# Weight conversion in the head: six one-input steps on GpSimd instead of VectorE, loads and head steps in another order

## The chip, the cores and the metric

The kernel runs on one core of a Trainium2 chip. The metric is the device time in microseconds (us) of one execution; smaller is better. TensorE (PE), VectorE (DVE), ScalarE (ACT), GpSimd (POOL) and SyncE (SP) each work through their own list of instructions in order; SP issues the transfers. A wait at the front of a list holds everything behind it.

## What is computed

An induced attention block over `x` (4 batches of 12544 tokens, 128 channels, float32), followed by a maxout layer with weights of 128 x 768. Cut to what matters:

```
def mab(q, kv):                      # softmax attention
    s = scale * (q @ kv.T); s -= s.max(-1)
    a = exp(s); a /= a.sum(-1) + 1e-9
    return a @ kv
h = mab(inducing, x)                 # 32 induced points per batch, over all 12544 tokens
y = mab(x, h)                        # every token against the 32 points
hid = maximum(maximum(y @ w1, y @ w2), y @ w3)
out = hid @ w_out
```

The four weights are float64. Each is brought to the chip as pairs of 32-bit words and converted there.

## The kernel before

**Two stages.** The *head* treats batch 0 up to the first products of the maxout layer; a main loop of slots follows, in which the maxout layer of one 512-token chunk after another is worked off while later batches' attention runs beside it. The order of every engine's instructions is that in which the code emits them; no scheduler changes it. In the head that order is the string `HEAD`: each word is a step, and a step appends its instructions to the lists of its engines.

**Loads.** The tokens of batch 0 come in seven groups: group 0 is short (2 tiles of 128 tokens), groups 1 to 6 have 16 tiles (1 MB) each. `LOADS` is the order in which SP issues them with the four weights (0.75 MB each; w_out is `wo`). Group 1 and group 6 are loaded in four pieces of 4 tiles.

**Head steps of batch 0.** For group g and piece k, `T:g.k` transposes four tiles on PE into a PSUM bank, `c:g.k` (ACT) or `C:g.k` (DVE) copies it to SBUF. `S:g` is the score product on PE, `M:g` its maximum (DVE), `D:g` spreads it (ACT), `G:g` sums it over partitions (PE), `L:g` takes the least (DVE), `E:g` the exponential (ACT), `R:g` a 32x32 transpose (DVE), `U:g` the product with the tokens (PE), `H:g` / `HV:g` its copy out of PSUM (ACT / DVE), `K:g` a copy of one column (POOL). Groups 0 and 1, 2 and 3, 5 and 6 share one maximum, so `G:5` waits for `M:6`. After the last group: `least`, `wts`, `lw` (the groups' weights), `maskp`, `y`, `tot`, `rec` and `hT`, the 32 induced points; from `hT` come the scores of the first chunks (`parts`, then the softmax steps `p:w.n`) and the first combined weights (`up`, `hi`, `lov`, `lop`).

**Weight conversion.** Weight k (0 is w2, 1 is w_out, 2 is w1, 3 is w3) passes through
`n:k` (ACT, absolute value of the high words), `r:k` (scale the low words), `m:k` (a lower bound), `i:k` (a shift by 3), `v:k` (POOL, integer sum of the two), `d:k` (DVE, put the sign back; two inputs from SBUF). `r`, `m` and `i` have one input and stand on DVE before. `e:k.part.parts` subtracts w2 from w1 or w3 on DVE, `ep` does it on POOL. The tiles of `n` (`size`) and of `r` (`rest`) have two buffers each, so the third weight's `r` waits for the first weight's `d`. `N` and `F` are products that nobody reads.

Of the kernel before, what the change touches and what calls it, by code (L numbers as in the profile page):

```python
# [26 lines left out]
def kernel(ctx, tc, x, xt, ind_t, w1, w2, w3, w_out, out):  # L27
    nc = tc.nc
    B, N, C = x.shape
    M = ind_t.shape[1]  # L30
# [15 lines left out]
    HEAD = """
        n:0 r:0 F:17 T:1.1 T:1.0 m:0 i:0 C:1.0 c:1.1 T:1.2 c:1.2 T:1.3 C:1.3 T:0.0 S:1 c:0.0 S:0 M:1 M:0 D:1 D:0 v:0
        d:0 T:2.2 C:2.2 T:2.3 c:2.3 T:2.0 c:2.0 G:1 L:1 K:0 T:2.1 C:2.1 E:1 T:3.3 E:0 c:3.3 T:3.2 T:3.0 c:3.0 T:3.1
        n:2 C:3.2 R:1 r:2 m:2 R:0 i:2 c:3.1 S:2 M:2 U:1 S:3 M:3 U:0 HV:1 T:4.1 C:4.1 v:2 D:2 D:3 T:4.2 c:4.2 G:2 L:2
        E:2 d:2 R:2 e:2.0.1 T:4.3 T:4.0 c:4.0 c:4.3 E:3 R:3 T:5.2 c:5.2 n:3 S:4 M:4 D:4 r:3 m:3 i:3 K:3 v:3 U:2  # L50
        T:5.0 c:5.0 T:5.1 c:5.1 G:4 L:4 E:4 T:5.3 C:5.3 T:6.0 C:6.0 T:6.2 c:6.2 T:6.1 c:6.1 R:4 T:6.3 c:6.3 S:5 d:3
        M:5 S:6 M:6 U:3 n:1 m:1 r:1 D:5 D:6 G:5 L:5 K:6 i:1 v:1 H:2 U:4 E:5 e:3.0.2 R:5 E:6 least R:6 H:4 w2T U:5
        U:6 wts lw maskp tot H:5 y:1 y:2 w2h d:1 woh wol y:4 y:5 rec hT parts:0 parts:2 e:3.1.2 p:0.0 p:0.1 p:0.2
        p:0.3 p:2.0 up:0 up:1 hi:0 hi:1 lop:1 p:0.4 p:0.5 p:2.1 p:0.6 p:0.7 up:2 hi:2 mw p:2.2 p:2.3 cw p:0.8 turn:0
        pca:0 turn:1 pca:1 lov:0 lov:2 p:2.4 s:0 up:3 hi:3 N:1 s:1 s:2 p:2.5 N:1 s:3 s:4 p:2.6 N:1 s:5 next p:2.7
        x:0 lov:3 s:6 p:2.8 q:0 q:1 x:1 q:2 q:3 q:4 q:5 q:6 q:7
    """
# [43 lines left out]
    def load_group(b, gi, pieces=1):
        g = groups[gi]
        if g["nt"] == GT:
            xg = xgs_free.pop(0) if xgs_free else xts_free.pop().rearrange("p (t c) -> p t c", c=C)
        else:
            xg = short_x
        n = g["nt"] // pieces
        for k in range(0, g["nt"], n):
            nc.sync.dma_start(out=xg[:, k : k + n, :], in_=xv[b, :, g["t0"] + k : g["t0"] + k + n, :])
# [73 lines left out]
    def weight_size(k):  # L183
# [5 lines left out]
    def weight_rest(k):
# [1 line left out]
        low = raws[k].rearrange("p (k two) -> p two k", two=2)[:, 0, :]
        nc.vector.tensor_scalar(out=rests[k], in0=low, scalar1=2.0**-51, scalar2=2.0, op0=ALU.mult, op1=ALU.add)

    def weight_least(k):
        nc.vector.tensor_scalar(out=sized[k], in0=sized[k], scalar1=LEAST, scalar2=None, op0=ALU.max)
# [973 lines left out]
```

## Time and profile before

| | |
|---|---|
| median of 3 runs | 809.62 us (809.48 to 809.74) |
| span of the profiled execution, first to last instruction | 807.8 us |
| what lies around the span | 1.85 us to the median; the profiled execution's own time is not listed apart |
| PE busy in the span | 799.0 us (99%) |
| DVE, ACT, POOL busy | 647.2, 714.4, 656.7 us (80%, 88%, 81%) |
| granted TensorE clock | 1.000 |
| head, to the first slots of the loop | about the first 48 us |

Idle time counts only on the engine that others wait for; of PE's idle time nearly all lies in the first 50 us. Times in the views are counted from the first instruction.

### The profile page before, as it was taken

To read this page: it belongs to the slowest core of one execution; us is meant where nothing else is said; L and a number is where in the kernel's file an instruction comes from. 1 tells how busy PE (TensorE), PEld (TensorE's weight loads), DVE (VectorE), ACT (ScalarE), POOL (GpSimd) and SP (SyncE) were. 2 spreads that over 40 slices of the span, in tenths; PEclk is the share of its full clock that TensorE was granted. 3 is DMA by queue.
4 is the path that set the end of the run, shared out by engine and by line. 5 is a ranking of instruction groups with operands and counts; after the bars stand their busy time and mean duration, and the time that the engine had idled before them with its cause. 6 is when DMAs were issued, how large, how long until landed. Compare 5 with 4: busy or idle time off the path is not lost.

```text
span 807.8 us, 15028 instructions
## 1 busy us (share of the span) xinstructions
PE 799.0 (99%) x4565; PEld 629.1 (78%) x4565; DVE 647.2 (80%) x1193; ACT 714.4 (88%) x1435; POOL 656.7 (81%) x637
## 2 busy tenths in 40 slices
PE   8999999999999999999999999999999999999998
PEld 6677778777787787787777877877778778777886
DVE  5988778779787797797976977978878878878874
...
GB/s 351 195 101 201 185 170 104 139 140 98 158 178 111 146 121 151 141 108 177 127 184 101 118 155 132 110 125 128 56 110 71 66 78 67 75 77 79 60 80 52
DMA packets 45408, 101.47 MB, mean 126 GB/s; under 512 B 9360, under 2 KB 15376, under 8 KB 40208
## 3 DMA queue, kind: packets, MB, share of 16 engines
...
q10 hardware_dynamic: 144, 0.13, 0.0%
...
## 4 chain that ended last, share of the span: by engine, by line
PE 95%; DMA 2%; ACT 1%; DVE 0%; issue 0%; SPq 0%; DVEq 0%
PE acc L942 50%; PE pu L848 16%; PE pv L854 16%; PE aux L730 3%; PE acc L936 3%; DMA xg<-in_x_dram 2%; PE acc L488 2%; PE aux L391 2%; PE aux L297 0%; PE acc L370 0%; PE aux L692 0%; ACT ru L863 0%; PE pv L281 0%; PE pu L281 0%; ACT a L336 0%
## 5 line engine op out<-in xcount | busy, mean ns | idle before, releaser
L878 POOL TENSOR_TENSOR lo<-h,hi 128x512 fp32r<-128x512 f32 (+1 forms) x498 | 621.2, 1277 | 111.3 <-ACT hi L870 54.7
L886 DVE TENSOR_TENSOR h<-pv,ru 128x512 f32<-128x512 f32 (+1 forms) x512 | 342.6, 672 | 129.3 <-PE pv L854 104.6
L863 ACT ACTIVATE ru<-pu 128x512 f32<-128x512 f32 (+1 forms) x600 | 368.2, 614 | 66.2 <-PE pu L848 61.9
L870 ACT CAST hi<-h 128x512 fp32r<-128x512 f32 (+1 forms) x512 | 320.1, 625 | 1.1 <-PE acc L942 0.7
L942 PE MATMUL acc<-hi,wo_hi 128*128 128x512 f32 (+1 forms) x601 | 234.8, 391 | 0.0
L848 PE MATMUL pu<-pT,us 128*128 128x512 f32 (+1 forms) x600 | 232.0, 387 | 0.3 <-ACT ru L863 0.2
L854 PE MATMUL pv<-pT,us 128*128 128x512 f32 (+1 forms) x600 | 231.6, 386 | 0.0
L942 PE MATMUL acc<-hi,wo_lo 128*128 128x512 f32 (+1 forms) x601 | 231.4, 385 | 0.0
L942 PE MATMUL acc<-lo,wo_hi 128*128 128x512 f32 (+1 forms) x601 | 231.3, 385 | 0.0
L942 PEld LDWEIGHTS acc<-hi,wo_hi 128*128 128x128 f32 x601 | 112.8, 188 | 41.3 <-issue 19.7
L848 PEld LDWEIGHTS pu<-pT,us 128*128 128x128 f32 x600 | 112.6, 188 | 24.3 <-issue 0.8
L854 PEld LDWEIGHTS pv<-pT,us 128*128 128x128 f32 x600 | 112.6, 188 | 23.5 <-DVE h L886 0.3
L942 PEld LDWEIGHTS acc<-lo,wo_hi 128*128 128x128 f32 x601 | 112.8, 188 | 22.9
L942 PEld LDWEIGHTS acc<-hi,wo_lo 128*128 128x128 f32 x601 | 112.9, 188 | 21.7
L886 DVE TENSOR_TENSOR aux<-pv,ru 128x512 f32<-128x512 f32 x66 | 45.7, 693 | 9.8 <-PE pv L854 3.5
L889 DVE TENSOR_TENSOR lo<-aux,hi 128x512 fp32r<-128x512 f32 x66 | 45.3, 686 | 1.4 <-PE acc L942 0.8
L870 ACT CAST hi<-aux 128x512 fp32r<-128x512 f32 x66 | 41.7, 632 | 0.1
L954 ACT COPY shelf<-acc 128x512 f32<-128x512 f32 (+1 forms) x65 | 39.1, 602 | 0.0
L936 PE MATMUL acc<-pT,us 128*128 128x512 f32 (+1 forms) x100 | 38.8, 388 | 0.0
L432 POOL COPY mq<-mq 32x1 f32<-32x1 f32 (+2 forms) x108 | 20.4, 189 | 5.2
L730 PE MATMUL aux<-xT,hT 128*32 128x512 f32 x184 | 24.5, 605 | 0.0
L488 PEld LDWEIGHTS acc<-xg,aT 128*32 128x32 f32 x576 | 16.8, 110 | 8.5 <-issue 7.8
...
## 6 DMA issues: line engine op xcount, KB each, us to landing
out_dram<-shelf SPq DMA_DIRECT2D x95, 256.0 KB, 2.0
...
```

What stands on the lines that cost most here:

```text
L488: nc.tensor.matmul(out=st["h"][q * M : (q + 1) * M, :], lhsT=aT[:, t * M : (t + 1) * M], rhs=row, start=(t < NQ), stop=(t + NQ >= len(rows)),)
L730: nc.tensor.matmul(out=sp[q * M : (q + 1) * M, :w], lhsT=st["hT"][:, :M], rhs=xT[:, q * w : (q + 1) * w], start=True, stop=True)
L848: nc.tensor.matmul(out=pu[:, :w], lhsT=state[c.b]["us"][:, 2 * j * P : (2 * j + 1) * P], rhs=c.pT[:, :w], start=True, stop=True)
L854: nc.tensor.matmul(out=pv[:, : d.w], lhsT=state[d.b]["us"][:, (2 * j + 1) * P : (2 * j + 2) * P], rhs=d.pT[:, : d.w], start=True, stop=True,)
L863: nc.scalar.activation(out=ru[:, :w], in_=pu[:, :w], func=AF.Relu)
L870: nc.scalar.copy(out=hi[:, : c.w], in_=h[:, : c.w])
L878: nc.gpsimd.tensor_sub(**args)
L886: nc.vector.tensor_max(out=h[:, : d.w], in0=pv[:, : d.w], in1=relus.pop(s)[:, : d.w])
L889: nc.vector.tensor_sub(**low)
L936: nc.tensor.matmul(out=c.acc[:, :w], lhsT=us[:, 2 * DF :], rhs=c.pT[:, :w], start=(base == 0), stop=False)
L942: nc.tensor.matmul(out=c.acc[:, cs], lhsT=lhs[:, j, :], rhs=rhs[j][:, cs], start=(j < base and j == 0 and lhs is wo_hi and rhs is c.hh), s ...
L954: (nc.vector.tensor_copy if by_vector else nc.scalar.copy)(out=o[:, : c.w], in_=c.acc[:, : c.w])
```

## The change

`LOADS` becomes a list of words in which the pieces of groups 1 and 6 and the attention's `ind` stand singly. Six of the eight `r` and `m` steps become `rp` and `mp`, the same instruction on GpSimd (`rp:2`, `rp:3`, `rp:1`, `mp:2`, `mp:0`, `mp:1`); `r:0` and `m:3` stay on VectorE. Both halves of w3's difference become `ep` (GpSimd); w1's stays on VectorE. `HEAD` is written anew. The new steps `w` and `wohp` are defined and not used.

```diff
-    LOADS = (0, 7, 1, 2, 3, 9, 4, 5, 10, 6, 8)
+    LOADS = """
+        x1.3 ind x1.0 x0 x1.2 x1.1 x2 x3 w1 x4 x5 w2 x6.0 w3 x6.2 x6.3 x6.1 wo
+    """
...
-        M:5 S:6 M:6 U:3 n:1 m:1 r:1 D:5 D:6 G:5 L:5 K:6 i:1 v:1 H:2 U:4 E:5 e:3.0.2 R:5 E:6 least R:6 H:4 w2T U:5
...
+        C:5.3 c:5.0 R:2 T:5.1 n:0 r:0 S:4 M:4 U:1 K:3 C:5.1 E:3 c:5.2 D:4 T:6.0 v:2 mp:0 G:4 U:0 c:6.0 i:0 n:3 L:4 S:5
+        E:4 HV:1 d:2 T:6.2 m:3 T:6.3 T:6.1 R:3 v:0 c:6.2 c:6.3 U:2 i:3 c:6.1 M:5 n:1 d:0 rp:3 D:5 S:6 M:6 v:3 U:3 R:4
...
-    def weight_rest(k):
+    def weight_rest(k, engine):
+        weight_words(k)
         rests[k] = hp.tile([P, DF], F32, name="rest", tag="rest", bufs=2)
-        nc.vector.tensor_scalar(out=rests[k], in0=low, scalar1=2.0**-51, scalar2=2.0, op0=ALU.mult, op1=ALU.add)
+        engine.tensor_scalar(out=rests[k], in0=words[k][0], scalar1=2.0**-51, scalar2=2.0, op0=ALU.mult, op1=ALU.add)
...
-    def weight_least(k):
-        nc.vector.tensor_scalar(out=sized[k], in0=sized[k], scalar1=LEAST, scalar2=None, op0=ALU.max)
+    def weight_least(k, engine):
+        engine.tensor_scalar(out=sized[k], in0=sized[k], scalar1=LEAST, scalar2=None, op0=ALU.max)
...
-            "r": weight_rest,
-            "m": weight_least,
+            "r": lambda k: weight_rest(k, vec),
+            "rp": lambda k: weight_rest(k, pool),
+            "m": lambda k: weight_least(k, vec),
+            "mp": lambda k: weight_least(k, pool),
```

On SP, the head's loads. Before (`shelf` is `ind` or group 0, `xg_86` to `xg_90` are groups 1 to 5, `xT_84` is group 6, the `raw` are w2, w1, w3 in this order):

```order
L517 DMA shelf<-in_ind_t_dram 128x32
L109 DMA shelf<-in_x_dram 128x256
L143 DMA raw<-in_w_dram 128x1536
L109 DMA xg_86<-in_x_dram 128x512 x4
L109 DMA xg_87<-in_x_dram 128x2048
L109 DMA xg_88<-in_x_dram 128x2048
L143 DMA raw<-in_w_dram 128x1536
L109 DMA xg_89<-in_x_dram 128x2048
L109 DMA xg_90<-in_x_dram 128x2048
L143 DMA raw<-in_w_dram 128x1536
L109 DMA xT_84<-in_x_dram 128x512 x4
L143 DMA raw<-in_w_out_dram 128x6x256
```

Now, from group 2 on (the `raw` are w1, w2, w3, w_out):

```order
L110 DMA xg_87<-in_x_dram 128x2048
L110 DMA xg_88<-in_x_dram 128x2048
L148 DMA raw<-in_w_dram 128x1536
L110 DMA xg_89<-in_x_dram 128x2048
L110 DMA xg_90<-in_x_dram 128x2048
L148 DMA raw<-in_w_dram 128x1536
L110 DMA xT_84<-in_x_dram 128x512
L148 DMA raw<-in_w_dram 128x1536
L110 DMA xT_84<-in_x_dram 128x512 x3
L148 DMA raw<-in_w_out_dram 128x6x256
```

The weight w2 has moved from the third place to behind group 5.

On POOL, the middle of the head. Before, from the second `v` on (L203 is `v`, L348 `K`, L622 `maskp`, L561 `wol`):

```order
L203 TENSOR_TENSOR rest<-rest,size 128x768
L348 COPY mneg<-mneg 128x1
L203 TENSOR_TENSOR rest<-rest,size 128x768
L348 COPY mneg<-mneg 128x1
L203 TENSOR_TENSOR rest<-rest,size 128x768
L622 TENSOR_TENSOR mask<-shelf,w 128x224
L561 TENSOR_TENSOR wo_lo<-xT_85,wo_hi 128x768
```

Now, from `v:2` on (L229 is `v`, L215 `mp`, L212 `rp`, L374 `K`, L245 `ep`, L651 `maskp`); the rows are `v:2 mp:0 v:0 rp:3 v:3 rp:1 mp:1 K:6 ep:3.1.2 maskp v:1 ep:3.0.2`:

```order
L229 TENSOR_TENSOR rest<-rest,size 128x768
L215 TENSOR_SCALAR size<-size 128x768
L229 TENSOR_TENSOR rest<-rest,size 128x768
L212 TENSOR_SCALAR rest<-raw 128x768
L229 TENSOR_TENSOR rest<-rest,size 128x768
L212 TENSOR_SCALAR rest<-raw 128x768
L215 TENSOR_SCALAR size<-size 128x768
L374 COPY mneg<-mneg 128x1
L245 TENSOR_TENSOR shelf<-dst,xT_85 128x3x128
L651 TENSOR_TENSOR mask<-shelf,w 128x224
L229 TENSOR_TENSOR rest<-rest,size 128x768
L245 TENSOR_TENSOR shelf<-dst,xT_85 128x3x128
```

Where three `v`, two `K` and `maskp` stood there are now also two `rp`, two `mp` and two `ep`.

On DVE, around the maxima of the last groups. Before, the rows are `d:3 M:5 M:6 m:1 r:1 L:5 i:1 e:3.0.2 R:5 least R:6 lw`:

```order
L207 SCALAR_TENSOR_TENSOR dst<-raw,rest 128x768
L307 TENSOR_REDUCE mq_402<-aux_71 128x1
L307 TENSOR_REDUCE mq_408<-aux_70 128x1
L195 TENSOR_SCALAR size<-size 128x768
L192 TENSOR_SCALAR rest<-raw 128x768
L329 TENSOR_REDUCE mneg<-acc_76 128x1
L199 TENSOR_SCALAR size<-size 128x768
L219 TENSOR_TENSOR shelf<-dst,xT_85 128x3x128
L355 STREAM_TRANSPOSE aT<-a 128x512
L613 TENSOR_REDUCE mmin<-mneg 128x1
L355 STREAM_TRANSPOSE aT<-a 128x512
L641 TENSOR_TENSOR lw<-w,lst 128x7
```

Now, `i:0 L:4 HV:1 d:2 m:3 R:3 i:3 M:5 d:0 M:6 R:4 L:5` stand there:

```order
L219 TENSOR_SCALAR size<-size 128x768
L355 TENSOR_REDUCE mneg<-acc_76 128x1
L407 COPY shelf<-acc_77 128x128
L233 SCALAR_TENSOR_TENSOR dst<-raw,rest 128x768
L215 TENSOR_SCALAR size<-size 128x768
L381 STREAM_TRANSPOSE aT<-a 128x512
L219 TENSOR_SCALAR size<-size 128x768
L333 TENSOR_REDUCE mq_393<-aux_71 128x1
L233 SCALAR_TENSOR_TENSOR xT_85<-raw,rest 128x768
L333 TENSOR_REDUCE mq_406<-aux_70 128x1
L381 STREAM_TRANSPOSE aT<-a 128x512
L355 TENSOR_REDUCE mneg<-acc_76 128x1
```

and behind them `d:3 R:5 least R:6 i:1 lw`, the sum of `lw`, `e:2.0.1`, `rec` (two instructions), `hT` and `d:1`:

```order
L233 SCALAR_TENSOR_TENSOR dst<-raw,rest 128x768
L381 STREAM_TRANSPOSE aT<-a 128x512
L642 TENSOR_REDUCE mmin<-mneg 128x1
L381 STREAM_TRANSPOSE aT<-a 128x512
L219 TENSOR_SCALAR size<-size 128x768
L670 TENSOR_TENSOR lw<-w,lst 128x7
L672 TENSOR_REDUCE l_514<-lw 128x1
L245 TENSOR_TENSOR shelf<-dst,xT_85 128x6x128
L680 TENSOR_SCALAR rec<-acc_76 128x32
L681 RECIPROCAL rec<-rec 128x32
L686 TENSOR_TENSOR hT<-pu_72,rec 128x128
L233 SCALAR_TENSOR_TENSOR xT_85<-raw,rest 128x768
```

The conversion of w2 (`i:0`, `d:0`), first of all before, now stands among the last groups, and a `d` stands ahead of `M:6` and of `R:5`.

## Rows read from the trace of the kernel before

**Rows 1.** Busy time by stretch: length, PE, PEld, DVE, ACT, POOL, clock, DMA, GB/s.
```profile
30.00:37.00 7.00, 6.10 (x142) 5.08 (x132) 6.46 (x16) 4.06 (x13) 2.98 (x3) 1.00 0.14 25
50.00:808.00 758.00, 754.27 (x4088) 594.99 (x4086) 608.06 (x1110) 680.90 (x1357) 639.07 (x616) 1.00 0.39 118
```

**Rows 2.** The chain that ended last: start us, us, what.
```profile
6.84 15.03 DMA xg<-in_x_dram
...
27.95 1.94 PE aux L297 x16
...
36.62 0.30 DVE hT L657
```

**Rows 3.** Load of group 6's last piece: its issue; us from issue to landing.
```profile
14.19 0.33 SPq L109 DMA_DIRECT2D xT<-in_x_dram  x1
...
xT<-in_x_dram SPq DMA_DIRECT2D x1, 256.0 KB, 12.2
```

**Rows 4.** Timeline of PE: start us, us, engine, line, tiles, form [idle before].
```profile
1.62 5.23 PE L273 MATMUL acc<-ident_r 128*128 128x384 f32 x17 [1.62 <-DVE ident_r L160]
...
7.76 1.07 PE L281 MATMUL pu<-shelf,xg 128*128 128x128 f32 x8 [0.91 <-DMA xg<-in_x_dram]
...
10.77 1.07 PE L297 MATMUL aux<-xT,shelf 128*32 128x512 f32 x8 [0.66 <-DVE xT L287]
```

**Rows 5.** Timeline of ACT: the `n` of a weight.
```profile
23.77 0.94 ACT L187 ACTIVATE size<-raw 128x768 f32<-128x768 f32 x1
```

**Rows 6.** DVE by line and form: count, us busy, mean ns, idle before.
```profile
L195 DVE TENSOR_SCALAR size<-size 128x768 f32<-128x768 f32 x4 | 2.2, 556 | 0.5 <-ACT size L187 0.5
L192 DVE TENSOR_SCALAR rest<-raw 128x768 f32<-128x768 uint32 x4 | 2.2, 544 | 4.0 <-DMA raw<-in_w_dram 4.0
...
L219 DVE TENSOR_TENSOR shelf<-dst,xT 128x768 f32<-128x768 f32 x1 | 0.9, 917 | 0.0
```

**Rows 7.** Timeline of POOL.
```profile
1.01 0.29 POOL masks.py:199 TENSOR_SCALAR_AFFINE_SELECT shelf<-shelf 128x128 f32<-128x128 f32 x1
...
14.32 0.18 POOL L348 COPY mneg<-mneg 128x1 f32<-128x1 f32 x1 [4.12 <-DVE mneg L329]
18.63 1.82 POOL L203 TENSOR_TENSOR rest<-rest,size 128x768 int32<-128x768 int32 x1 [4.13 <-DVE size L199]
20.78 0.85 POOL L348 COPY mneg<-mneg 128x1 f32<-128x1 f32 x1 [0.33 <-DVE mneg L329]
...
32.22 2.02 POOL L203 TENSOR_TENSOR rest<-rest,size 128x768 int32<-128x768 int32 x1
34.19 0.57 POOL L622 TENSOR_TENSOR mask<-shelf,w 128x224 f32<-128x224 f32 x1
```

**Rows 8.** Timeline of DVE.
```profile
20.64 0.95 DVE L207 SCALAR_TENSOR_TENSOR dst<-raw,rest 128x768 uint32<-128x768 uint32 x1
...
29.91 0.69 DVE L307 TENSOR_REDUCE mq<-aux 128x1 f32<-128x512 f32 x1 [0.21 <-PE aux L297]
...
31.45 0.16 DVE L329 TENSOR_REDUCE mneg<-acc 128x1 f32<-128x8 f32 x1
...
31.99 0.55 DVE L219 TENSOR_TENSOR shelf<-dst,xT 128x384 f32<-128x384 f32 x1
...
33.13 0.71 DVE L355 STREAM_TRANSPOSE aT<-a 128x512 f32<-128x512 f32 x1
33.76 0.50 DVE L641 TENSOR_TENSOR lw<-w,lst 128x7 f32<-128x7 f32 x1
34.30 0.16 DVE L643 TENSOR_REDUCE l<-lw 128x1 f32<-128x7 f32 x1
34.37 1.20 DVE L207 SCALAR_TENSOR_TENSOR xT<-raw,rest 128x768 uint32<-128x768 uint32 x1
35.71 0.19 DVE L651 TENSOR_SCALAR rec<-acc 128x32 f32<-128x32 f32 x1
```

More of the change, by code (lines that the diff above doesn't have):

```diff
@@ L46 @@
     HEAD = """
[L47 to L51, printed above, removed]
-        M:5 S:6 M:6 U:3 n:1 m:1 r:1 D:5 D:6 G:5 L:5 K:6 i:1 v:1 H:2 U:4 E:5 e:3.0.2 R:5 E:6 least R:6 H:4 w2T U:5
[L53 to L56, printed above, removed]
+        F:17 T:1.3 T:1.2 T:1.0 c:1.0 T:1.1 T:0.0 C:1.3 c:1.1 C:1.2 S:1 T:2.3 C:0.0 M:1 S:0 T:2.0 M:0 D:1 D:0 G:1 C:2.0
+        T:2.2 C:2.2 T:2.1 C:2.1 T:3.2 T:3.1 L:1 T:3.0 E:0 E:1 C:2.3 T:3.3 C:3.1 C:3.0 c:3.2 c:3.3 R:1 R:0 S:2 S:3 M:3
+        T:4.3 n:2 T:4.2 D:3 M:2 T:4.0 c:4.3 C:4.0 D:2 T:4.1 G:2 rp:2 c:4.2 T:5.3 mp:2 T:5.0 i:2 L:2 E:2 C:4.1 K:0 T:5.2
+        C:5.3 c:5.0 R:2 T:5.1 n:0 r:0 S:4 M:4 U:1 K:3 C:5.1 E:3 c:5.2 D:4 T:6.0 v:2 mp:0 G:4 U:0 c:6.0 i:0 n:3 L:4 S:5
+        E:4 HV:1 d:2 T:6.2 m:3 T:6.3 T:6.1 R:3 v:0 c:6.2 c:6.3 U:2 i:3 c:6.1 M:5 n:1 d:0 rp:3 D:5 S:6 M:6 v:3 U:3 R:4
+        D:6 G:5 rp:1 H:2 L:5 U:4 d:3 mp:1 w2T K:6 E:5 R:5 least H:4 U:5 E:6 R:6 wts w2h i:1 U:6 ep:3.1.2 maskp lw
+        e:2.0.1 H:5 y:1 tot y:2 y:4 y:5 rec hT v:1 N:1 d:1 parts:0 woh p:0.0 p:0.1 parts:2 p:0.2 ep:3.0.2 p:0.3 p:2.0
+        up:2 p:0.4 up:1 up:0 hi:2 p:0.5 p:0.6 p:2.1 hi:1 p:2.2 p:0.7 p:0.8 mw hi:0 wol turn:0 lop:1 p:2.3 turn:1 cw
+        lov:0 lov:2 p:2.4 pca:0 pca:1 s:0 p:2.5 s:1 s:2 s:3 s:4 p:2.6 up:3 s:5 next x:0 p:2.7 s:6 q:0 N:1 hi:3 p:2.8 q:1
+        x:1 N:1 q:2 q:3 q:4 q:5 lov:3 q:6 q:7
     """
@@ L98, with space_for, load_tiles, load_group @@
     xv = x.rearrange("b (p t) c -> b p t c", t=NT)
[L101 to L109, printed above, removed]
+    def space_for(gi):
+        if groups[gi]["nt"] < GT:
+            return short_x
+        return xgs_free.pop(0) if xgs_free else xts_free.pop().rearrange("p (t c) -> p t c", c=C)
+    def load_tiles(b, gi, xg, a, z):
+        t0 = groups[gi]["t0"]
+        nc.sync.dma_start(out=xg[:, a:z, :], in_=xv[b, :, t0 + a : t0 + z, :])
+    def load_group(b, gi):
+        xg = space_for(gi)
+        load_tiles(b, gi, xg, 0, groups[gi]["nt"])
         return xg
@@ L144, in load_raw @@
         return r
-    srcs = [w2.bitcast(U32), w_out.bitcast(U32).rearrange("(j p) c -> p j c", p=P), w1.bitcast(U32), w3.bitcast(U32)]
+    srcs = {
+        "w2": (0, w2.bitcast(U32)),
+        "wo": (1, w_out.bitcast(U32).rearrange("(j p) c -> p j c", p=P)),
+        "w1": (2, w1.bitcast(U32)),
+        "w3": (3, w3.bitcast(U32)),
+    }
     raws = {}
-    FULLS = [gi for gi in LOADS if 0 < gi < NG]
+    SPARE_HOME = NG - 1
     def first_loads():
-        for what in LOADS:
-            if what < NG:
-                state[0]["xg"][what] = load_group(0, what, pieces=4 if what in (FULLS[0], FULLS[-1]) else 1)
-            else:
-                raws[what - NG] = load_raw(srcs[what - NG])
+        xgs = state[0]["xg"]
+        xgs.update({gi: space_for(gi) for gi in range(NG)})
+        for what in LOADS.split():
+            if what == "ind":
+                nc.sync.dma_start(out=iT, in_=ind_t)
+            elif what in srcs:
+                k, src = srcs[what]
+                raws[k] = load_raw(src)
+            else:
+                gi, piece = ([int(n) for n in what[1:].split(".")] + [None])[:2]
+                a, z = (0, groups[gi]["nt"]) if piece is None else (4 * piece, 4 * piece + 4)
+                load_tiles(0, gi, xgs[gi], a, z)
     ident = place(P)
@@ L181, with weight_words, weight_size @@
     words, sized, rests, floats = {}, {}, {}, {}
[L183 removed]
+    def weight_words(k):
         v = raws[k].rearrange("p (k two) -> p two k", two=2)
         words[k] = v[:, 0, :], v[:, 1, :]
+    def weight_size(k):
+        weight_words(k)
         sized[k] = hp.tile([P, DF], F32, name="size", tag="size", bufs=2)
         nc.scalar.activation(out=sized[k], in_=words[k][1].bitcast(F32), func=AF.Abs)
[L189 removed]
+    def weight_rest(k, engine):
+        weight_words(k)
         rests[k] = hp.tile([P, DF], F32, name="rest", tag="rest", bufs=2)
[L191 to L195 removed]
+        engine.tensor_scalar(out=rests[k], in0=words[k][0], scalar1=2.0**-51, scalar2=2.0, op0=ALU.mult, op1=ALU.add)
+    def weight_least(k, engine):
+        engine.tensor_scalar(out=sized[k], in0=sized[k], scalar1=LEAST, scalar2=None, op0=ALU.max)
     def weight_shift(k):
@@ L199, in weight_shift, with weight_join @@
         nc.vector.tensor_scalar(out=bits, in0=bits, scalar1=3, scalar2=None, op0=ALU.logical_shift_left)
+    def weight_join(k):
+        whole = rests[k].bitcast(I32)
+        nc.gpsimd.scalar_tensor_tensor(
+            out=whole, in0=sized[k].bitcast(I32), scalar=8, in1=whole, op0=ALU.mult, op1=ALU.add
+        )
     def weight_whole(k):
@@ L360, in attend_sums @@
         st = state[b]
-        xg, aT = st["xg"].pop(gi), st["a"].pop(gi)
+        xg, aT = st["xg"][gi], st["a"].pop(gi)
         members = JOINT[LEADER[gi]]
-        if gi == FULLS[-1]:
+        if gi == SPARE_HOME:
             xts_free.append(xg.rearrange("p t c -> p (t c)"))
@@ L516, in head @@
         start_batch(0)
-        nc.sync.dma_start(out=iT, in_=ind_t)
+        first_loads()
         nc.scalar.mul(out=iT, in_=iT, mul=scale)
-        first_loads()
         st = state[0]
@@ L554, in head @@
             "n": weight_size,
-            "r": weight_rest,
-            "m": weight_least,
+            "r": lambda k: weight_rest(k, vec),
+            "rp": lambda k: weight_rest(k, pool),
+            "m": lambda k: weight_least(k, vec),
+            "mp": lambda k: weight_least(k, pool),
             "i": weight_shift,
+            "w": weight_join,
             "v": weight_whole,
             "d": weight_sign,
-            "woh": lambda: nc.scalar.copy(out=wo_hi, in_=wo),
+            "woh": lambda: act.copy(out=wo_hi, in_=wo),
+            "wohp": lambda: pool.tensor_copy(out=wo_hi, in_=wo),
             "wol": lambda: nc.gpsimd.tensor_sub(out=wo_lo, in0=wo, in1=wo_hi.bitcast(F32)),
@@ L665, in first_products @@
     def first_products(st, which, bank):
-        if which == 0:
+        if "us" not in st:
             st["us"] = bp.tile([P, UW], F32R, name="us", tag="us")
```

## The prediction

> **What bounds the kernel now.** First the busy time by stretch [rows 1]: from 50 us on PE is busy 754 of 758 us, and the list of waits has none of PE's in that stretch. What the head loses or gains is therefore carried to the end one for one; in the head PE falls short (6.10 of 7 us between 30 and 37), while DVE is busy 6.46. Second the chain that ended last [rows 2]: transfers up to 21.87 us (group 5 lands), then PE and the attention of the last groups to `hT` at 36.62, from which everything later starts. So the question is when `hT` starts. Between the last score products (27.95, two groups together) and `hT` lie `M:6` at 29.91, `L:5` at 31.45, `R:6` at 33.13 and `rec` at 35.71, all on DVE [rows 8]. These four times are the milestones of the sum.
>
> **Loads.** SP issues as many loads as before, in another order, and no later transfer is moved past another. The stream is full, so I take a transfer to land when the bytes ahead of it are through. Ahead of w2 and with it now stand `ind`, groups 0 to 5, w1 and w2: exactly the set that had landed with group 5 before. So w2 lands at 21.87 [rows 2] instead of early enough for the first conversion. The set up to group 6's last piece is also the same: 14.19 + 12.2 = 26.39, as before [rows 3]. w3 comes one piece of group 6 later than it did, still ahead of that piece; nothing on the path below waits for it. At the front group 1 comes first, and `ind` behind its first piece. The unread products `F` hold PE until 6.85, the first transposes waited for a load until 7.76, and `S:1` started at 10.77 [rows 4]: 3.0 us after the first transposes. Now they can start when `F` ends and `S:1` at 6.85 + 3.0 = 9.9 or, as later pieces are awaited no more, up to half a microsecond sooner. This lead of about 1 us is real and is lost again where group 2, w2 and group 6 are awaited.
>
> **What leaves DVE and what it costs on GpSimd.** Six instructions of 0.55 us, 3.3 us in all [rows 6], and two half differences of 0.55 [rows 8]: 4.4 us off DVE. GpSimd's price for a one-input instruction on 768 elements is not in the trace. Lower bound: 128 elements took 0.29 and a single one 0.18 [rows 7], so 0.18 + 768 x 0.11 / 127 = 0.84. Upper bound: the two-input sum of the same size, 1.82 [rows 7]. I take 0.9, near the row with one input. The page "GPSIMD Engine Reference" of the Trainium skill, section "Engine selection", calls one-input work there roughly line rate and two-input work about twice as slow as VectorE, which is the same choice; no run here shows it yet.
>
> **What it costs DVE.** The price that decides is not GpSimd's own. Where `d` (two inputs from SBUF) met a GpSimd instruction, one waited for the other. `K` took 0.85 instead of 0.18 because `d:2` ran to 21.59 [rows 7, 8]. `v:1` started at 32.22 inside the difference that ran to 32.54, and took 2.02 instead of 1.82. The other way round, `lw` on 7 columns (its sum takes 0.16) took 0.50 and ended at 34.26, when `v:1` ended at 34.24; and `d:1` took 1.20 instead of 0.95 because `maskp` ran to 34.76: it ended 0.81 after it. So whoever comes second waits for the whole of the first, and a blocked `d` ends 0.81 after the holder. Before, a `d` mostly follows its own `v`, with GpSimd idle. Now GpSimd's list is nearly always full. The page "SBUF — State Buffer" of the Trainium skill, section "Who interferes with whom", has this as a rule: the port pair goes to whoever issues first for the whole instruction, and the other fully blocks. By the rule a blocked `d` would end its whole 0.95 after the holder, 0.14 later than the rows have it; for the four blocks below that adds 0.6 us.
>
> **The chain, step by step.**
> - *w2 to `i:0`.* 21.87 landed; `n:0` 0.94 [rows 5]; `mp:0` 0.9; `i:0` 0.55, like the other one-input steps; 0.05 to 0.1 at each handover: `i:0` ends at 24.45. DVE's own queue (`M:4`, `C:5.1`) reaches `i:0` at about 23.8 and hides nothing of it.
> - *`d:2` behind `v:0`.* `v:0` takes GpSimd from 24.5 to 26.35. On DVE only `L:4` and `HV:1` (0.5 us) stand between `i:0` and `d:2`, so `d:2` is blocked wherever the chain lies: it ends at 26.35 + 0.81 = 27.15.
> - *To `M:6`.* `m:3` 0.5, then `rp:3` on GpSimd (it needs the buffer that `d:2` frees) beside `R:3` 0.7; `i:3` just behind both, to 28.8. `v:3` runs from 28.9 to 30.7; only `M:5` (0.69) stands between `i:3` and `d:0`, so `d:0` is blocked again and ends at 31.5. `M:6` is behind it: 31.5 instead of 29.91, +1.6. Group 6's scores are ready by then (the last piece landed at 26.39, `S:6` near 28).
> - *To `R:6`.* `M:6` to `L:5` is 1.54 as before: 33.0. Between `L:5` and `R:5` DVE had two instructions of 0.55; now it has `d:3`, held up by `mp:1` until about 33.35: 34.2. ACT's copy `H:4` now also precedes `E:6`. `R:6` starts at about 35.1, +2.0.
> - *To `hT`.* `R:6` ends at 35.8; `i:1` 0.55, `lw`. `v:1` starts as soon as `i:1` ends and holds `e:2.0.1` (0.92, [rows 6]) for 1.82: it ends at 36.45 + 1.82 + 0.78 = 39.0. `rec` is behind `e:2.0.1`, and `rec` to `hT` is 36.62 - 35.71 = 0.91: `hT` at 39.95, +3.3. Without the block `e:2.0.1` would end near 37.4 and `hT` start at 38.3, +1.7.
> - *After `hT`.* `d:1` (0.95) now stands ahead of the first softmax step, where `e:3.1.2` (0.55) stood beside a wait for PE; against that the first softmax's division no longer waits behind two steps of the second. I take 0. `wol` and `lop` come as much later on GpSimd as their inputs; nobody waits for them sooner.
>
> **Sum.** 3.3 us on the span of 807.8; nothing around the span changes, so also on the median: 809.62 + 3.3 = 812.9. If the one-input price is 1.82, `mp:0` is 0.9 later and `rp:3` holds `i:3` another 1.0: 814.8. If `v:1` comes after `e:2.0.1`, 809.62 + 1.7 = 811.3. That is the likeliest case's own range, 811.3 to 814.8.
>
> **Rivals.** The bound for a change that can be told from none is 0.2%, 1.6 us.
> - *Same: GpSimd's work costs DVE nothing.* Without the blocks `d:2` ends at 26.2, `d:0` at 29.45, `M:6` starts at 29.45 (0.45 early), `L:5` at 31.0; `H:4` ahead of `E:6` on ACT takes that back, `R:6` is where it was, and `i:1`, `lw` and `e:2.0.1` (1.8 us together) put `rec` at 35.65. Time 809.6, between 808.2 and 811.2. For it speaks that both lists have slack early; against it the two blocked DVE instructions above. It also takes the case in which one or two blocks are missed.
> - *Faster: the lead is kept.* DVE has 4.4 us less and the last group is alone: its transposes end near 27.0 (half a microsecond behind the last piece), `S:6` starts at 27.2 instead of 27.95 for two groups, and `M:6` at 28.2 instead of 29.91. Kept to `hT`, 1.7 us: 807.9. It decides from `M:6` at 28.3 or earlier. Against it: `d:0` stands ahead of `M:6` and needs w2, which lands at 21.87, and `n:0`, `mp:0`, `i:0`, `v:0` one after the other.
> - *Slower by the one-input price alone.* If GpSimd needed 1.82 and nothing blocked, `i:0` would end at 25.35 and `M:6` be 0.5 late: still within 1.6 us. So the price alone does not decide, the blocks do.
>
> **How the numbers follow.** The forecast, blocks at `d:2`, `d:0` and `e:2.0.1`, 0.66; the rival without them, with the slow price in it, 0.24; the kept lead 0.10. Nearly all of the forecast's range is above 811.2, so slower by over 0.2% is 0.66, within it 0.24, faster 0.10. The range goes from 808.6, which leaves out the kept lead and a part of the second case, to 814.8, the upper bound of the price.
>
> **What would show it.** In the changed kernel: w2's load landing near 21.9 and the last piece of group 6 near 26.4; `rp` and `mp` at 0.84 to 1.82 on GpSimd; `d:2`, `d:0`, `e:2.0.1` at well over 0.95 (or DVE idle before them) and ending 0.8 after a GpSimd instruction; `M:6` near 31.5, `hT` near 40; no waits of PE from 52 us on. It is wrong if those three keep their 0.95 while GpSimd works, if `v` steps start late enough to leave DVE the way, or if the loads come in a faster order than their bytes say.

## The result

The changed kernel takes 818.06 us (median of 4 runs, 817.26 to 820.28); the kernel before, run beside it, 809.55 (809.44 to 809.74). The ratio is 1.0108, 95% interval 1.0093 to 1.0122: 0.9 to 1.2% slower. The profiled execution, one of the four, took 817.26 us with a span of 815.5, 7.7 more than before.

The profile of the changed kernel, in the order in which it answers the rows of before. Busy time by stretch, as [rows 1]; the column that reads 0.57, 0.88 and 1.00 is the granted clock, a mean over the stretch:

```profile
28.00:32.00 4.00, 4.00 (x46) 3.50 (x48) 4.00 (x5) 2.90 (x6) 2.47 (x3) 0.57 0.09 29
30.00:37.00 7.00, 5.58 (x112) 4.03 (x111) 6.81 (x10) 3.58 (x9) 5.40 (x4) 0.88 0.00 0
52.00:815.00 763.00, 759.97 (x4115) 597.65 (x4114) 612.30 (x1120) 686.03 (x1369) 643.56 (x621) 1.00 0.38 117
```

PE is still full behind the head (760 of 763 us), and nothing in the list of waits is PE's there. New is a stretch of 3.4 us at 0.5 of the clock (1.2 GHz) from 28.3 us on; PE had been idle for 1.69 us up to 26.58. The chain that ended last goes through the three steps that the forecast named (L233 is `d:2`, then `d:0`, whose wait counts as "issue"; L245 is `e:2.0.1`):

```profile
23.43 0.92 PE acc L396 x32
27.56 2.42 DVE dst L233
32.22 0.98 DVE xT L233
33.21 1.13 issue
...
39.69 2.37 DVE shelf L245
```

w2's load, against [rows 2, 3] (issue on SP, then size and time to landing), and PE's `S:1`, `U:1`, `G:4` (with its wait) and `S:6`, against [rows 4]:

```profile
6.62 0.65 SPq L148 DMA_DIRECT2D raw<-in_w_dram  x1
```
```profile
raw<-in_w_dram SPq DMA_DIRECT2D x1, 768.0 KB, 16.5
```
```profile
10.15 1.06 PE L323 MATMUL aux<-xT,shelf 128*32 128x512 f32 x8
...
23.25 1.06 PE L396 MATMUL acc<-xg,aT 128*32 128x128 f32 x32
...
26.58 0.39 PE L349 MATMUL acc<-md,shelf 128*128 128x4 f32 x2 [1.69 <-ACT md L342]
...
32.07 1.03 PE L323 MATMUL aux<-xT,shelf 128*32 128x512 f32 x8
```

w2 lands at 6.62 + 16.5 = 23.1. GpSimd's timeline, against [rows 7] (L229 is `v`, L215 `mp`, L212 `rp`, L651 `maskp`):

```profile
24.16 2.13 POOL L215 TENSOR_SCALAR size<-size 128x768 f32<-128x768 f32 x1 [1.04 <-ACT size L207]
27.34 1.82 POOL L229 TENSOR_TENSOR rest<-rest,size 128x768 int32<-128x768 int32 x1 [1.05 <-DVE mneg L355]
30.14 1.07 POOL L212 TENSOR_SCALAR rest<-raw 128x768 f32<-128x768 uint32 x1 [0.97 <-POOL rest L229]
31.77 1.83 POOL L229 TENSOR_TENSOR rest<-rest,size 128x768 int32<-128x768 int32 x1 [0.56 <-DVE size L219]
...
35.34 2.12 POOL L215 TENSOR_SCALAR size<-size 128x768 f32<-128x768 f32 x1
...
38.52 0.95 POOL L651 TENSOR_TENSOR mask<-shelf,w 128x224 f32<-128x224 f32 x1
39.44 1.80 POOL L229 TENSOR_TENSOR rest<-rest,size 128x768 int32<-128x768 int32 x1
```

And DVE's, against [rows 8]: `R:2 r:0 M:4 C:5.1 i:0`, then `d:2`, `i:3 M:5 d:0 M:6`, `L:5 d:3`, `R:6`, `e:2.0.1`, `hT`, and one instruction of the loop.

```profile
24.44 0.71 DVE L381 STREAM_TRANSPOSE aT<-a 128x512 f32<-128x512 f32 x1 [2.15 <-PE acc L396]
25.07 0.52 DVE L212 TENSOR_SCALAR rest<-raw 128x768 f32<-128x768 uint32 x1
25.51 0.68 DVE L333 TENSOR_REDUCE mq<-aux 128x1 f32<-128x512 f32 x1
26.11 0.68 DVE L313 COPY xT<-pu 128x512 f32<-128x512 f32 x1
26.71 0.55 DVE L219 TENSOR_SCALAR size<-size 128x768 uint32<-128x768 uint32 x1
...
27.56 2.42 DVE L233 SCALAR_TENSOR_TENSOR dst<-raw,rest 128x768 uint32<-128x768 uint32 x1
...
31.00 0.63 DVE L219 TENSOR_SCALAR size<-size 128x768 uint32<-128x768 uint32 x1
31.55 0.68 DVE L333 TENSOR_REDUCE mq<-aux 128x1 f32<-128x512 f32 x1
32.15 2.27 DVE L233 SCALAR_TENSOR_TENSOR xT<-raw,rest 128x768 uint32<-128x768 uint32 x1
34.34 0.68 DVE L333 TENSOR_REDUCE mq<-aux 128x1 f32<-128x512 f32 x1
...
35.82 0.17 DVE L355 TENSOR_REDUCE mneg<-acc 128x1 f32<-128x8 f32 x1 [0.19 <-PE acc L349]
35.91 1.06 DVE L233 SCALAR_TENSOR_TENSOR dst<-raw,rest 128x768 uint32<-128x768 uint32 x1
...
37.90 0.71 DVE L381 STREAM_TRANSPOSE aT<-a 128x512 f32<-128x512 f32 x1
...
39.61 2.45 DVE L245 TENSOR_TENSOR shelf<-dst,xT 128x768 f32<-128x768 f32 x1
...
43.07 0.29 DVE L686 TENSOR_TENSOR hT<-pu,rec 128x128 f32<-128x128 f32 x1 [0.53 <-DVE rec L681]
...
425.31 0.69 DVE L915 TENSOR_TENSOR h<-pv,ru 128x512 f32<-128x512 f32 x1 [0.30 <-POOL lo L907]
```

Read them in pairs. `d:2` starts at 27.56, inside `v:0` (27.34 to 29.16), and ends at 29.98, 0.82 after it. `d:0` (32.15 to 34.42) ends 0.82 after `v:3`, `e:2.0.1` (39.61 to 42.06) 0.82 after `v:1`. `hT` is 6.45 us later than before; the loop's first cast `hi` (ACT) 6.38 later; between 422 and 545 us another 1.3 us is lost. That is the span's 7.7.

### The profile page after: what moved, and what is told of

The parts are those of the page before. It is cut to its first block, busy times and chain, and to the rows that moved or that the text cites. A ratio compares the mean times of both kernels' runs of the same rounds, so it can differ in the third digit from the quotient of the medians.

```text
span 815.5 us, 15052 instructions
## 1 busy us (share of the span) xinstructions
PE 803.9 (99%) x4565; PEld 630.2 (77%) x4565; DVE 650.3 (80%) x1190; ACT 712.5 (87%) x1430; POOL 667.4 (82%) x645
## 4 chain that ended last, share of the span: by engine, by line
PE 96%; DVE 2%; ACT 1%; issue 0%; POOL 0%; POOLq 0%; DVEq 0%
PE acc L971 50%; PE pv L883 17%; PE pu L877 17%; PE aux L759 3%; PE acc L965 3%; PE acc L514 2%; PE aux L417 2%; PE acc L299 1%; PE pv L307 1%; PE aux L323 1%; PE pu L307 0%; PE aux L721 0%; DVE dst L233 0%; DVE shelf L245 0%; DVE mq L333 0%
## 5 line engine op out<-in xcount | busy, mean ns | idle before, releaser
L514 PEld LDWEIGHTS acc<-xg,aT 128*32 128x32 f32 x576 | 16.8, 110 | 8.5 <-issue 7.8
## 6 DMA issues: line engine op xcount, KB each, us to landing
raw<-in_w_dram SPq DMA_DIRECT2D x3, 768.0 KB, 16.5
```

What stands on the lines that cost most here:

```text
L514: nc.tensor.matmul(out=st["h"][q * M : (q + 1) * M, :], lhsT=aT[:, t * M : (t + 1) * M], rhs=row, start=(t < NQ), stop=(t + NQ >= len(rows)),)
```

## The experiments

Diffs are cut, and are of the changed kernel unless the text says otherwise.

**Take the six steps back, or make them alone.** First the changed kernel with the six on DVE again (one line of its edit below), then the kernel before with nothing but the six moved:

```diff
-        G:2 rp:2 c:4.2 T:5.3 mp:2
+        G:2 r:2 c:4.2 T:5.3 m:2
```

> The changed kernel with the six one-input steps back on VectorE (loads, order and the GpSimd differences as changed). Theory A, the blocks: VectorE's two-input steps wait for whole GpSimd sums, and the sums stay where they are, so d:2 and e:2.0.1 are still held some 1.4 us each: 816 to 818.5 us. Theory B, the price: the bound step takes 2.1 us on GpSimd and 0.55 on VectorE, and lies on the chain to i:0, so the time falls by about 2 to 3 us: 814.5 to 816.

Measured: 818.46 us (818.31 to 818.64), ratio 1.0105 (1.0090 to 1.0120), as theory A has it. `d:2` took 2.52 behind `v:0`, `e:2.0.1` 2.59 behind `v:1`; `hT` at 44.41.

> The kernel before with only the six one-input steps moved to GpSimd, at the same places of its order, loads as before. Theory A: a block needs a GpSimd sum beside a VectorE two-input step, which the order before hardly has, so little is lost: 809.5 to 811 us. Theory B: the bound step of w1 holds the shift, and behind it on VectorE two maxima, by about 1.6 us, and w_out's holds the shift ahead of R:5: 811 to 813.5 us.

Measured: 812.63 us (812.48 to 812.76), ratio 1.0034 (1.0022 to 1.0046); theory B's range. GpSimd's `mp:2` and `mp:1` of this run:

```profile
17.75 2.13 POOL L215 TENSOR_SCALAR size<-size 128x768 f32<-128x768 f32 x1 [0.64 <-ACT size L207]
...
31.56 2.12 POOL L215 TENSOR_SCALAR size<-size 128x768 f32<-128x768 f32 x1 [1.92 <-ACT size L207]
```

and `i:2` and `i:1`, which wait for them on DVE:

```profile
19.91 0.56 DVE L219 TENSOR_SCALAR size<-size 128x768 uint32<-128x768 uint32 x1 [3.03 <-POOL size L215]
...
33.72 1.33 DVE L219 TENSOR_SCALAR size<-size 128x768 uint32<-128x768 uint32 x1 [0.22 <-POOL size L215]
```

`i:1` took 1.33 instead of 0.55 because `rp:1`, now behind `mp:1`, ran from 33.65 to 34.63; it ended 0.42 after it. `hT` starts at 39.77, 3.15 late, and the loop carries that unchanged to the end. So the six steps cost 2.8 us in the order of before, and nothing more in the new order, which is slow without them.

**The multiply-adds alone**, in the kernel before:

```diff
-        n:2 C:3.2 R:1 r:2 m:2 R:0
+        n:2 C:3.2 R:1 rp:2 m:2 R:0
```

> The kernel before with the three rp alone on GpSimd, m on VectorE, loads and order of before. With all six it was 2.8 us slower. Theory M (the maxima were dear, the multiply-adds are hidden where GpSimd idles): hT within 0.4 us of before (36.62), total 809.2 to 810.4. Rival (any one-input step on GpSimd holds DVE up by its length on the path): hT 1 us late or more, 810.8 to 812.5.

Measured: 809.54 us (809.03 to 810.0), ratio 0.9997 (0.9988 to 1.0006); `hT` at 36.71. The three `rp` (0.92 to 0.96) alone are hidden, as theory M has it. What the six cost comes with the `mp`, but some 0.8 of the 3.15 us passes through `rp:1` on `i:1` (above), and no run has the `mp` alone. In the changed kernel the same split gives nothing:

> The changed kernel with its three mp (2.13 us each on GpSimd) back on VectorE (0.55), rp left on GpSimd (0.92). Theory M (the price of mp is what the forecast missed, through v:0 that starts after it and K:6 that stands behind mp:1): M:6 about 33.1 instead of 34.34, hT 41.5 to 42.5 instead of 43.07, total 816.2 to 817.5. Rival M2 (DVE pays the same in its place): as with all six back, 817.8 to 818.8.

Measured: 818.27 us (817.9 to 818.91); rival M2. `M:6` at 35.78, `hT` at 44.77: the maxima now stand in DVE's own list, and the blocked `d:2` and `e:2.0.1` take 2.53 and 2.59.

**Why `mp` is dear.** Three other forms in its place, a single run:

```diff
+            "ma": ... scalar1=1.0, scalar2=0.0, op0=ALU.mult, op1=ALU.add),
+            "mb": ... scalar1=LEAST, scalar2=1.0, op0=ALU.max, op1=ALU.mult),
+            "mc": ... scalar1=1.0, scalar2=None, op0=ALU.mult),
```

> The changed kernel with its three mp (maximum with a constant, one operation, in place, 2.13 us each on GpSimd; rp, multiply and add from the raw words, takes 0.92) in three other forms, in place on the same tiles: mp:2 becomes multiply by 1 and add 0; mp:0 becomes maximum and multiply by 1; mp:1 becomes multiply by 1 alone. mp:2 and mp:1 leave the maximum out. Theory P1 (the maximum is dear): 0.9, 2.1, 0.9. Theory P2 (the form with one operation is dear): 0.9, 0.9, 2.1. Theory P3 (float input in place is dear): 2.1 three times. Time under P1 or P2 between 816 and 818.5.

```profile
18.17 0.83 POOL L584 TENSOR_SCALAR size<-size 128x768 f32<-128x768 f32 x1 [1.66 <-ACT size L207]
24.58 2.78 POOL L585 TENSOR_SCALAR size<-size 128x768 f32<-128x768 f32 x1 [1.36 <-ACT size L207]
...
36.05 2.14 POOL L586 TENSOR_SCALAR size<-size 128x768 f32<-128x768 f32 x1
```

Measured: 817.85 us, and none of the three patterns. Multiply and add takes 0.83 in place, a lone multiply 2.14, maximum and multiply 2.78 (one instance each). So it is neither the maximum alone nor the form with one operation alone; of the forms tried only multiply and add is cheap. Why this is so stays open.

**Take the locks away.** The integer sum becomes two fills of the same tile, which read nothing (the sum is left out, so the weights lack their high words):

```diff
-        nc.gpsimd.tensor_tensor(out=whole, in0=whole, in1=sized[k].bitcast(I32), op=ALU.add)
+        nc.gpsimd.memset(sized[k], 2.0)
+        nc.gpsimd.memset(sized[k], 2.0)
```

> The changed kernel with each integer sum on GpSimd replaced by two fills of the shifted tile (the sum is left out, so the weights lack their high words); the fills wait for the same shift and should take about as long together, but read nothing from SBUF. Theory A, in the form that the sum's reads hold the two-input steps: d:2, d:0 and e:2.0.1 take 0.95 each and 4 us go: 813 to 814.5 us. If GpSimd's place in the chain and not its reads is what costs, 816.5 to 818.5 us and the three steps still at 2.3 us or idle before them.

Measured: 814.17 us (812.71 to 814.44), 3.9 less than the changed kernel.

```profile
26.85 0.54 DVE L219 TENSOR_SCALAR size<-size 128x768 uint32<-128x768 uint32 x1
...
27.69 0.95 DVE L234 SCALAR_TENSOR_TENSOR dst<-raw,rest 128x768 uint32<-128x768 uint32 x1
...
31.09 0.94 DVE L234 SCALAR_TENSOR_TENSOR xT<-raw,rest 128x768 uint32<-128x768 uint32 x1
33.38 0.69 DVE L334 TENSOR_REDUCE mq<-aux 128x1 f32<-128x512 f32 x1 [1.35 <-PE aux L324]
...
38.35 0.95 DVE L246 TENSOR_TENSOR shelf<-dst,xT 128x768 f32<-128x768 f32 x1
```

All three steps are back at 0.95, though the first fill (27.45 to 28.19) lay beside `d:2`. `hT` starts at 40.08, 3.0 earlier. But 3.5 us of the delay stay: `i:0` ends 0.1 later than it did, and `M:6` now waits 1.35 us for PE, whose clock was granted at 0.5 for most of 28 to 32 us in this run too.

**The same locks, met by order alone:** `d:2` ahead of `i:0`, `d:0` ahead of `i:3`, `e:2.0.1` ahead of `i:1`.

```diff
-  ... v:2 mp:0 G:4 U:0 c:6.0 i:0 n:3 L:4 S:5 E:4 HV:1 d:2 T:6.2 m:3
+  ... v:2 mp:0 G:4 U:0 c:6.0 d:2 i:0 n:3 L:4 S:5 E:4 HV:1 T:6.2 m:3
```

> The changed kernel with three two-input DVE steps moved ahead of the shift that releases the next integer sum: d:2 ahead of i:0, d:0 ahead of i:3, e:2.0.1 ahead of i:1; same work on every engine. Theory A (the sums lock those three steps out): d:2, d:0 and e:2.0.1 at about 0.95 us each, M:6 about 1 us and hT 2 to 3.5 us earlier than in the changed kernel (34.34, 43.07), total 814.5 to 816.5. Rival A2 (the sums lock out whatever DVE step stands there, or the loads alone set these times): M:6 and hT within 0.7 us of the changed kernel, 817.4 to 818.8.

Measured: 820.29 us (819.0 to 820.75), above both ranges. The three steps take 0.94, 1.05 and 0.92, and `M:6` starts at 33.31, 1.0 earlier. `hT` does not (43.25). `v:0` (28.27 to 30.08) now holds the next DVE step, a one-input maximum, and `mp:1` starts inside `d:3`, takes 2.83 and holds `K:6` and with it `least`:

```profile
28.38 2.12 DVE L215 TENSOR_SCALAR size<-size 128x768 f32<-128x768 f32 x1
```
```profile
35.36 2.83 POOL L215 TENSOR_SCALAR size<-size 128x768 f32<-128x768 f32 x1
```

A second stretch at half the clock, from 44.1 to 47.5 us, lies under the first products: `hT` is 6.6 late, the first casts 8.1.

**The loads.** The changed kernel with the loads of before, then with only the first five words in another order (`ind x0 x1.3 x1.0 x1.2 x1.1`):

> The changed kernel with the loads in the order of before (w2 third, group 1 after it). Theory C, the loads: w2 landing at 23.1 us sets n:0, mp:0 and i:0; with w2 near 6 us all of this moves up by about 1.2 us, and the first scores come 1.5 to 2 us later but wait behind nothing: 816.3 to 817 us. Theories A and B: R:2 and the maximum of group 4 hold VectorE until 26.7 anyway, so within 0.6 us of the changed kernel, 817.2 to 818.5 us; last piece of group 6 near 26.4 us if the order itself made the stream slower, near 27.8 us if not.

Measured: 821.22 us (821.13 to 821.85), outside the ranges of all three theories; `hT` at 47.25. The new head order needs the new load order, which gives it 3 us. The run shows what holds `i:0`:

```profile
29.85 0.67 DVE L313 COPY xT<-pu 128x512 f32<-128x512 f32 x1
30.45 0.54 DVE L219 TENSOR_SCALAR size<-size 128x768 uint32<-128x768 uint32 x1
```

w2 had landed at 6.3 and `mp:0` had ended at 28.92, yet `i:0` follows `C:5.1` without a pause; `R:2`, at the head of that queue, had again waited 2.14 us for `U:1`. Theory C is wrong. The stream moved 409 GB/s between 4 and 10 us, and the last piece of group 6 landed at 26.7, so it is the order of the loads that slows the stream.

> The changed kernel with the first load words in another order, ind x0 x1.3 x1.0 x1.2 x1.1 instead of x1.3 ind x1.0 x0 x1.2 x1.1, the rest as changed. In the changed kernel x2 took 3.9 us to land after group 1 where every other group takes 2.5, and w2 landed at 23.10 instead of 21.87. Theory F1 (the short loads between group 1's pieces slow the front): x2 lands 2.5 to 2.9 us after group 1, w2 at 21.8 to 22.3. Rival F2 (it comes from what is in flight behind the front, or of the first microseconds as such): w2 at 22.8 to 23.3. Total within 1.5 us of the changed kernel either way.

Measured: 817.56 us (817.0 to 817.74). w2 landed at 22.3 (6.70 + 15.6), 0.8 earlier, which is within F1's limits; group 2 landed 3.0 us behind group 1, just outside them. `mp:0` ended at 25.49 instead of 26.29, and yet:

```profile
25.82 0.67 DVE L333 TENSOR_REDUCE mq<-aux 128x1 f32<-128x512 f32 x1
26.42 0.68 DVE L313 COPY xT<-pu 128x512 f32<-128x512 f32 x1
27.02 0.54 DVE L219 TENSOR_SCALAR size<-size 128x768 uint32<-128x768 uint32 x1
```

`i:0` starts at 27.02, right behind `C:5.1`, 0.3 later than in the changed kernel. It waits neither for w2 nor for the result of `mp:0`. But `mp:0` reaches it by way of the queue: `r:0` (25.04 to 25.90) took 0.86 instead of 0.52 and ended 0.41 after `mp:0`.

**DVE's list ahead of `i:0`.** `U:1` earlier on PE, then the same with the maxima on DVE:

```diff
-  ... C:5.3 c:5.0 R:2 T:5.1 n:0 r:0 S:4 M:4 U:1 K:3 C:5.1
+  ... C:5.3 c:5.0 U:1 R:2 T:5.1 n:0 r:0 S:4 M:4 K:3 C:5.1
```

> The changed kernel with U:1 two steps earlier on PE, ahead of group 5's last transposes and S:4; R:2 on DVE waited for it until 24.4 us (two buffers of aT), and M:4 and i:0 stand behind R:2. Theory Q (i:0 is held twice, by DVE's queue behind R:2 and by mp:0 that ends at 26.29): R:2 at about 22.8 instead of 24.44, but i:0 only at 26.3 to 26.4 instead of 26.71, M:6 0.2 to 0.6 us earlier than 34.34. Rival Q2 (the queue alone holds it): i:0 at 25.7 or sooner, M:6 at 33.4 or sooner.

> Both: U:1 early as in the run beside it, and the three mp back on VectorE as in an earlier run, which alone gave nothing. Theory Q (either alone leaves the other): i:0 at 26.0 or sooner, d:2 ends near 29.0 instead of 29.98, M:6 33.0 to 33.6 and hT 41.5 to 42.5 instead of 43.07. Rival Q3 (w2's late landing at 23.1 and the conversion's steps behind it set M:6 either way): M:6 at 34.0 or later.

Measured: 816.97 us (816.77 to 817.47) and 817.27 (816.71 to 817.82). In the first `R:2` starts at 23.73, `i:0` at 26.44 and `M:6` at 34.12. Theory Q has `M:6` right and `i:0` nearly, but not `R:2` (22.8 expected) and not the reason, since `mp:0` had ended at 26.07 and `i:0` followed `C:5.1`; `S:4`, now behind `U:1` on PE, held `M:4`. In the second `i:0` starts at 26.79 and `M:6` at 34.42: Q3's number, but the runs with w2 landing earlier have ruled its reason out. What stays in all of them is the list `R:2 r:0 M:4 C:5.1`, fed by PE's `U:1` and `S:4`. No run takes it from ahead of `i:0`, so what it costs alone was not measured.

**The clock.** Six unread products ahead of `G:4` (`F:6`):

> The changed kernel with six more unread products ahead of G:4, which take PE through the idle stretch of 24.9 to 26.6 us, behind which its granted clock was 0.50 (1.2 GHz) for 3.4 us. Theory K1 (the low clock costs nothing here, DVE sets M:6 and hT): no change, 817.3 to 818.6. Rival K2 (the low clock costs what PE loses in it, up to 1.7 us): granted clock 1.00 throughout and 816.2 to 817.0.

Measured: 818.04 us (817.39 to 819.49): no change, K1.

```profile
28.00:32.00 4.00, 4.00 (x80) 3.02 (x80) 4.00 (x5) 3.06 (x6) 2.47 (x3) 1.00 0.10 33
36.00:40.00 4.00, 4.00 (x65) 3.27 (x68) 3.06 (x7) 2.72 (x8) 3.26 (x4) 0.57 0.00 0
```

The stretch is gone where it was, and another stands at 36.0 to 39.4, so the clock was not 1.00 throughout and K2 was not tried in full. There it counts: `R:6` waited 0.92 us for ACT, which waited for PE, and started 4.37 us after `M:6` instead of 3.56.

**The loss after 422 us.** Whose is it? First the old end of the head behind `hT`:

> The changed kernel up to hT, and from there the head's end of the kernel before (first softmax steps, first products, first slots in the old order; both halves of w3's difference stay on GpSimd). It tells where the further 1.3 us come from that the changed kernel loses between 422 and 545 us, long after the head. Theory D1 (the order at the head's end sets where the loop's engines stand to each other): the first casts are 6 to 6.8 us late as in the changed kernel and stay so to the end, 815.8 to 816.9. Rival D2 (a start that is late by so much does it by itself): they drift by over 1 us again, 817.4 to 818.8.

Measured: 819.14 us (817.43 to 819.95); casts 8.3 late at first (with a half-clock stretch at 44.0 to 47.4), 9.5 from 560 us on: D1 is wrong. D2 is not enough either: with the six alone the casts started 3.1 late and nothing more was lost, without the locks they started 3.7 late and 1.2 more was lost. In the changed kernel and all its versions above, with first casts 3.7 to 10.6 late, 1.2 to 1.4 us went between 415 and 546 us, whatever the lateness. The programs' own lists show a difference. The instruction that starts at 418.66 before and at 425.31 after:

```
L886 TENSOR_TENSOR h<-pv_74,ru 128x512 [waits PE_49,Activation_49]
L915 TENSOR_TENSOR h<-pv_74,ru 128x512 [waits PE_49,Activation_49,Pool_49]
```

The step list of the loop is the same; the tiles lie elsewhere in SBUF, since they take what earlier tiles have freed, and this `h` now waits for GpSimd's `lo` as well. Before, it had not paused (compare the line at 425.31 above):

```profile
418.66 0.68 DVE L886 TENSOR_TENSOR h<-pv,ru 128x512 f32<-128x512 f32 x1
```

Two runs move only the tiles, by a buffer tag of their own; the first:

```diff
-            w2h = hp.tile([P, 512], F32, name="w2h", tag="ru", bufs=3)
+            w2h = hp.tile([P, 512], F32, name="w2h", tag="w2h", bufs=2)
```

> The changed kernel with the same instructions in the same order; only the two tiles of w2's transposed copy get buffers of their own, so that tiles of the loop come to lie elsewhere in SBUF. In the changed kernel the place of the loop's tiles differs from before, and the maximum h of the loop waits for GpSimd's lo in 24 places where it did not (in 17 others no more), among them the one at 425.3 us with which the further loss begins. Here those waits near 410 to 540 us are as before. Theory P (the place of the tiles makes the further loss): first casts 6 to 7 us late as in the changed kernel, less than 0.5 us more at the end, 816.2 to 817.4. Rival P2 (the late start makes it): 1.0 to 1.6 us more between 422 and 545 us, 817.4 to 818.8.

> The same again with another place: the exponential and its transpose in the head get buffers of their own. h waits for GpSimd in 57 other places of the loop and no more in 58, spread over the whole loop. Theory P: the loss behind the first casts is another one than 1.3 us in the changed kernel by at least 0.5 us, of either sign, and comes in another place. Rival P2: 1.0 to 1.6 us between 422 and 545 us, 817.4 to 818.8.

Measured: 818.51 us (817.27 to 818.63) and 820.85 (819.79 to 821.27). In the first the casts are 8.0 late, 0.1 more up to 560 us and then 0.8 more by 780 us; the same `h` no longer waits:

```profile
426.59 0.68 DVE L915 TENSOR_TENSOR h<-pv,ru 128x512 f32<-128x512 f32 x1
```

In the second they are 8.0 late and lose another 3.1, from 150 to 560 us. With the same instructions in the same order the loss came to 1.3, 0.9 and 3.1 us, in other places: theory P. Two of P's numbers were missed in the first run: 0.9 instead of under 0.5 was lost behind the first casts, and the total is above its range, since the first casts were 8.0 late (a second half-clock stretch, 44.9 to 48.3 us). The waits in the traces go with the losses: `h` waits for GpSimd where it did not before in 24 places of the changed kernel (389 to 566 us), in 5 of the first run (665 to 783), in 57 of the second (109 to 787), and in none with the six alone.

## Why the prediction was wrong

The direction and the blocks were right, the size was not: +3.3 us forecast, +8.5 measured by the medians, outside the range. By its steps:

- **Blocks: right.** `d:2`, `d:0` and `e:2.0.1` were each held by the sum that was named and ended 0.82 after it (forecast 0.81). With the sums reading nothing, `hT` came 3.0 us earlier: shown. The Trainium skill, "SBUF — State Buffer", section "Who interferes with whom", says that a DVE step with two SBUF inputs contends with a GpSimd instruction that reads SBUF and not with one that only writes; the fills agree (0.95 beside them). `d:3`, which started 0.57 us into `mp:1`, does not: it took 1.06. Nor did a blocked step end its whole 0.95 after the holder, as the prediction reads this rule, but 0.82.
- **"DVE's own queue (`M:4`, `C:5.1`) reaches `i:0` at about 23.8 and hides nothing of it": this step failed.** The queue reached `i:0` at 26.71, so it ended 2.8 us after the forecast 24.45, and `M:6` came 2.8 us after the forecast 31.5. `R:2` waited 2.15 us for PE's `U:1` (the transposed weights `aT` have two buffers) and took `r:0`, `M:4` and `C:5.1` along. The prediction gives no working for 23.8: I took the queue's time from the old order without following PE's new one. That w2's landing (23.1 for 21.87) does not set it is shown by the runs with w2 0.8 and 16.8 us earlier, and that `mp:0` as the input of `i:0` does not, by the same two (it had ended 1.5 us before `i:0` began in each). That the 2.8 us would go with the queue is argued: `U:1` two steps earlier brought `R:2` forward by 0.7 and `i:0` by 0.3.
- **"`S:6` near 28": wrong too, and hidden here.** `S:6` started at 32.07, behind `G:4`, which had waited 1.69 us for the spread of `M:4`, and a half-clock stretch. `d:0` ended later still. In the run without the locks `M:6` waited 1.35 us for it, so the blocks alone do not set `M:6`.
- **One-input price: mis-sized.** `rp` took 0.87 to 1.07 (forecast 0.9), `mp` 2.13, above the bound of 1.82. With the `mp` the six cost 2.8 us in the order of before, without them nothing; in the new order the `mp` cost nothing net. "Roughly line-rate" for one input (the Trainium skill, "GPSIMD Engine Reference", section "Engine selection") is near `rp` (0.92 for 0.54 on DVE) and not `mp` (2.13 for 0.56).
- **Loads: wrong by 1.2 us for w2 and 1.4 for the last piece of group 6 (27.8), without effect on `i:0`.** The stream moved 323 GB/s between 4 and 10 us instead of 405. The order of the first words gives 0.8 back; what the rest is stays open.
- **`M:6` to `hT`: right to 0.3.** `M:6` to `R:6` 3.56 (forecast 3.6); `R:6` to `hT` 5.17 (4.85), in part because `maskp`, held by `i:1`, delayed `v:1`.
- **After `hT`: 0 held to the first casts (6.45, then 6.38 late); "carried to the end one for one" did not.** The tiles' places, and with them the waits for `lo`, cost 1.3 us more. The sum: 3.3 + 2.8 + 0.3 - 0.1 + 1.3 = 7.6 of the span's 7.7.
- **The clock** was not in the forecast (0.5 of 2.4 GHz is the lower level, 1.2). In the profiled run `M:6` waited for `d:0` and not for PE, so its stretch was not on the path. In other places it is: in the three profiles with a stretch between 44 and 48 us (locks met by order, old end of the head, w2's copy in its own buffers) `hT` to the first cast took 9.6 to 9.7 us instead of 8.06. The other three runs of the changed kernel took 817.65 to 820.28 at mean clocks of 0.995 to 0.998 instead of 1.000; that these 0.4 to 3 us are such stretches is argued, as no profile shows them. For the same reason differences of about 1 us between versions of the changed kernel rank none of them.
- **Rivals.** Without the locks the change is still 4.4 us slower than before (814.17 against 809.8), so "same" was wrong for reasons it did not name: the queue, PE behind it, and the loop's loss. No version tried is faster than before; `rp` alone equals it.
